# Chunked retention ahead of two feed-forward layers: k is loaded once and turned on TensorE, the lo parts of the converted weights move to VectorE, and the conversion gets a new pace

## The chip, the cores and the metric

The kernel runs on one core of a Trainium2 chip. The metric is device time in microseconds (us). The kernel before has a median of 803.65 us over 3 runs (802.65 to 805.5). Times below that come from the trace belong to one more, profiled execution of the same program, which took 802.34 us, 800.3 us of it in the profiled span.

## The reference

What is computed, cut to what matters:

```python
# 1 attention: 4 batches, 8 heads, 576 positions, head size 64; the decay replaces a softmax
ret = (q @ k.T / 8) * where(i >= j, gamma[h] ** (i - j), 0)
x   = (ret @ v)                      # laid out as 2304 tokens x 512
# 2 a gated product of two projections; the weights come as float64
x   = ((x @ w_a) * (x @ w_b)) @ w_out          # 512 -> 1536 -> 512
# 3 a mixture of 8 experts, one expert for each token
e   = argmax(x @ w_gate + modality_bias[modality_id])
out = softmax_weight * (relu(x @ w1[e]) @ w2[e])    # 512 -> 1024 -> 512
```

## The kernel before, in words

Every engine works off a list whose order is that of the code (the scheduler is off). Big tiles are `unit`s of 4 KB in each of the 128 partitions, of which there are 40, and a load on SyncE's queue (SP) waits until the unit that it gets is free. PSUM has 8 banks.

**Attention** goes over 20 chunks of 64 or 128 positions (5 for each batch: one of 64, then four of 128), with a state that is carried from chunk to chunk. For chunk i, `a_load` fetches `qk` (q and k, both already transposed on the host) and `kv` (k and v as rows, so k comes twice). `a_scale` on GpSimd (POOL) multiplies q and k by decays. `a_scores` on TensorE (PE) makes the scores, `a_mask` on VectorE (DVE) writes the carried state times a decay into a block-diagonal tile `sbd` (L358) and multiplies the scores by the decay mask (L366), `a_inter`, `a_state` and `a_intra` on PE make the output and the next state, and `a_hi`/`a_lo` write the output out of PSUM. One pass of the loop, here called a step, holds the scores of chunk i+1 and everything else of chunk i. The first steps hold `warm`, matmuls on constants.

**Conversion.** The weights of part 2 are float64; a piece is 128 x 512 of them, and there are 36 (w_a, w_b and w_out for each of 12 groups fc). `Conv.step(new)` moves each piece under way on by one stage and starts `new` others. The stages: load (SP); nothing; absolute value on ScalarE (ACT, L262); four instructions on DVE that put a float32 together from the two halves (L265, L269, L273, L277; called the four below); the hi part on ACT (L284, rounded to float32r) and the lo part, value minus hi, on POOL (L285). The attention steps named in `CV_AT` start one piece each, 8 in all; from then on each step of part 2 starts two (`CV_MOE`), over 14 steps.

**Part 2** goes in steps of one token group (384 tokens) and one fc. In a step `gemm1` makes two products in PSUM (L565), the first of which ACT copies out (`a`); DVE multiplies the second by it (`g`, L573), ACT rounds that (`gh`), DVE subtracts (`gl`, L577); `gemm2` of the step before follows on PE (L585). The first two token groups alternate (8 fc each), so the pieces are used as they are converted. Their six accumulators leave two PSUM banks, so the second product of a step can't start before `g` of the step before it has been read out. Hooks in the steps issue conversion, set-up (`setup` at step 1) and the routing weights (`load_gate` at step 18).

Of the kernel before, what the change touches and what calls it, by code (L numbers as in the profile page):

```python
# [9 lines left out]
F32 = mybir.dt.float32  # L10
# [40 lines left out]
def _const_parts():  # L51
    g = 1.0 - 2.0 ** (-5.0 - np.arange(H))
    i = np.arange(P)
    rel = i[None, :] - i[:, None]
    mask = np.where(
        rel[:, None, :] >= 0,
        g[None, :, None] ** np.maximum(rel, 0)[:, None, :],
        0.0,
    ) / np.sqrt(D)
    mask = mask.reshape(P, NP, 2, P).transpose(0, 2, 1, 3)  # L60
    gp = np.repeat(g.reshape(NP, 2).T, D, axis=0)
    qt = gp[:, :, None] ** i[None, None, :] / np.sqrt(D)
    kt = np.zeros((P, 5, H))
    st = np.zeros((P, 5, NP))
    for c, s0 in enumerate(STARTS):
        kt[:, c, :] = g[None, :] ** (-(s0 + i)[:, None].astype(float))
        st[:, c, :] = gp ** float(s0)
    one = np.ones((P, 1))
    parts_a = [("mask", mask), ("kt", kt), ("st", st), ("qt", qt)]
    parts_b = [  # L70
        ("tri", (rel > 0).astype(float)),
        ("ident", np.eye(P)),
        ("iota8", one * np.arange(NE)[None, :]),
        ("base0", one * (np.arange(NE) * NTOK)[None, :]),
        ("tok", i[:, None] + P * np.arange(NTT)[None, :]),
        ("thr0", one * (NT * np.arange(7) + NS)[None, :]),
        ("thr1", one * (NT * np.arange(7))[None, :]),
        ("sid", one * (np.arange(MAXS) - EARLYS * 1.0)[None, :]),
        ("jp", i[:, None] + P * np.arange(TPC)[None, :]),
    ]  # L80
    return parts_a, parts_b
# [18 lines left out]
def build(  # L100
    ctx: ExitStack,
    tc: tile.TileContext,
    qkf,
    kv,
    wab,
    wout,
# [46 lines left out]
    def unit(name, shape, dt=F32):  # L153
        return up.tile(shape, dt, name=name, tag="u")
# [44 lines left out]
            nc.tensor.matmul(ps, lhsT=ones, rhs=wide, start=True, stop=True)  # L199

    def setup():
        nc.sync.dma_start(out=cb, in_=cstb)
        nc.gpsimd.tensor_copy(tri, cb_("tri"))
        nc.gpsimd.tensor_copy(base, cb_("base0"))

        zt = unit("zt", [P, NE * NTT * 2])
        nc.gpsimd.memset(zt, 0.0)
        nc.gpsimd.dma_start(out=perm.rearrange("(p a) o -> p (a o)", p=P), in_=zt)


# [21 lines left out]
    class Conv:  # L232
# [23 lines left out]
        def advance(self, c):  # L256
            c["n"] += 1
            i, raw = c["i"], c["raw"]
            fc, j = divmod(i, 3)
            if c["n"] == 2:  # L260
                t = c["t"] = unit(f"cv{i}", [P, 512], U32)
                nc.scalar.activation(out=t.bitcast(F32), in_=raw[:, :, 1].bitcast(F32), func=AF.Abs)  # L262
            elif c["n"] == 3:
                t = c["t"]
                nc.vector.tensor_scalar(  # L265
                    out=t.bitcast(F32), in0=t.bitcast(F32), scalar1=k1, scalar2=k2,
                    op0=ALU.max, op1=ALU.min,
                )
# [12 lines left out]
            elif c["n"] == 4:  # L281
                t = c["t"]
                w = wts[fc][j] = unit(f"w{fc}_{j}", [P, 2, 512], F32R)
                nc.scalar.copy(w[:, 0, :], t.bitcast(F32))  # L284
                nc.gpsimd.tensor_sub(w[:, 1, :], t.bitcast(F32), w[:, 0, :].bitcast(F32))  # L285
                self.live.remove(c)


# [8 lines left out]
        return [xp.tile([P, KC, NT], F32, name=f"xf{n}", tag="x")]  # L297

    chunks = [(b, c) for b in BATCHES for c in range(5)]
    offs = np.cumsum([0] + [P * 8 * SIZES[c] for b, c in chunks])  # L300
    A = [dict() for _ in chunks]

    def geo(i):
        b, c = chunks[i]
        return b, c, SIZES[c], b * S + STARTS[c]

    def a_load(i, what=("qk", "kv")):
        b, c, n, r0 = geo(i)
        if "qk" in what:
            qk = unit(f"qk{i}", [P, 2 * NP * P])[:, : 2 * NP * n]  # L310
            nc.sync.dma_start(
                out=qk, in_=qkf[int(offs[i]) : int(offs[i + 1])].rearrange("(p f) -> p f", p=P)
            )
            A[i]["qk"] = qk.rearrange("p (t a s) -> p t a s", t=2, a=NP)
        if "kv" in what:
            A[i]["kv"] = unit(f"kv{i}", [P, 2, DM])
            nc.sync.dma_start(
                out=A[i]["kv"][:n], in_=kv[r0 : r0 + n, :].rearrange("r (t d) -> r t d", t=2)
            )

    def a_scale(i):
        b, c, n, r0 = geo(i)
# [2 lines left out]
        A[i]["qs"] = qks[:, 0, :].rearrange("p (a s) -> p a s", a=NP)  # L325
        A[i]["ks"] = qks[:, 1, :]
        if c > 0:
            nc.gpsimd.tensor_mul(A[i]["qs"][:, :, :n], qk[:, 0, :, :n], qt[:, :, :n])
        if c < 4:
            nc.gpsimd.tensor_mul(  # L330
                qks[:n, 1, :].rearrange("p (h d) -> p h d", h=H),
# [19 lines left out]

    def a_mask(i):
        b, c, n, r0 = geo(i)
        if c > 0:
            A[i]["S"] = sbd[i % 2]
            for hf in range(2):
                sl = slice(D * hf, D * hf + D)
                nc.vector.tensor_mul(  # L358
                    sbd[i % 2][sl, :, sl],
                    A[i - 1]["Sp"][sl, :, :],  # L360
                    st[sl, c, :].unsqueeze(2).to_broadcast([D, NP, D]),
                )
        rt = unit(f"rt{i}", [P, 2, NP, P])
        A[i]["rt"] = rt
        for hf in range(2):
            nc.vector.tensor_mul(  # L366
                rt[:n, hf, :, :n], A[i]["sc"][hf][:n, :, :n], mask[:n, hf, :, :n]
            )

    def a_state(i):  # L370
        b, c, n, r0 = geo(i)
# [73 lines left out]
    n_ch = len(chunks)
    a_load(0, ["qk"])
    a_load(1, ["qk"])
    a_load(0, ["kv"])
# [740 lines left out]
```

## Time and profile before

| | |
|---|---|
| time, median of 3 runs | 803.65 us (802.65 to 805.5) |
| the profiled execution's own time | 802.34 us |
| its span | 800.3 us |
| PE busy | 755.3 us (94%) |
| DVE busy | 492.0 us (61%) |
| ACT busy | 245.1 us (31%) |
| POOL busy | 200.1 us (25%) |

The shares of busy time are means over parts with different limits: attention lies at the start (some 87 us), conversion beside the first steps of part 2 follows (to about 219 us), then part 2 without conversion, then the experts. A share of 94% for PE says little of either of the first two.

### The profile page before, as it was taken

Reading aid. Unit: us, or ns where it says so; the run is one execution under the profiler, and the core shown is the slowest. Engines: PE = TensorE matmul, PEld = TensorE weight load, DVE = VectorE, ACT = ScalarE, POOL = GpSimd, SP = SyncE. Lnnn points to the kernel's source line nnn. Section 1 sums busy time; section 2 is a strip of 40 time slices with the busy share of each in tenths; the row PEclk is TensorE's granted clock in tenths of the full one; section 3 lists DMA queues with packets and bytes.
Section 4 is the critical chain, followed back from the end, with each engine's and each line's share of the span. In section 5 each row is a group of like instructions: output and inputs, shape, how many; then the busy total and the mean of one; then the engine's idle time right before and its main releaser. Section 6 shows DMA issues by size and latency. Waiting matters only on the chain.

```text
span 800.3 us, 12194 instructions
## 1 busy us (share of the span) xinstructions
PE 755.3 (94%) x4610; PEld 686.1 (86%) x4610; DVE 492.0 (61%) x1212; ACT 245.1 (31%) x461; POOL 200.1 (25%) x213
## 2 busy tenths in 40 slices
PE   8888999878899999999999999999999999999992
PEld 6777998767798899999999999999978999999992
DVE  3799458989839664454445545856896844444610
ACT  1232233334321311221122112215434435344621
POOL 4576313424213210030003000113115133140302
PEclk9999999999999999999999999999999999999997
DMA  9999702322041100100020001034746385465201
GB/s 323 400 364 409 247 25 82 106 81 77 1 185 39 41 1 1 45 36 0 1 80 1 1 1 39 2 101 151 288 139 152 101 295 168 131 200 160 80 1 44
DMA packets 27908, 91.99 MB, mean 115 GB/s; under 512 B 4543, under 2 KB 4703, under 8 KB 27840
## 3 DMA queue, kind: packets, MB, share of 16 engines
q1 hardware_dynamic: 22928, 79.11, 28.6%
q0 software_dynamic: 4336, 9.92, 4.0%
q10 hardware_dynamic: 576, 2.10, 0.7%
q8 instruction: 38, 0.62, 0.3%
q14 instruction: 30, 0.25, 0.1%
HBM read 78.36 MB, written 13.01 MB: 114 GB/s over the span
## 4 chain that ended last, share of the span: by engine, by line
PE 65%; DVE 18%; issue 7%; DMA 5%; POOL 1%; ACT 1%; SPq 1%; POOLq 0%; DVEq 0%; ACTq 0%
PE ab L565 30%; PE acc L585 15%; PE h L849 9%; PE y L866 9%; DVE cv L273 4%; DVE cv L269 3%; DMA raw<-in_wab_dram 3%; DMA qk<-in_qkf_dram 2%; DVE scr L502 2%; DVE cv L265 1%; DVE cv L277 1%; DVE g L573 1%; DVE el L783 1%; ACT gh L575 1%; DVE gl L577 1%
## 5 line engine op out<-in xcount | busy, mean ns | idle before, releaser
L565 PE MATMUL ab<-xh,w 128*128 128x384 f32 x1152 | 277.5, 337 | 16.2 <-DVE g L573 14.2
L565 PEld LDWEIGHTS ab<-xh,w 128*128 128x128 f32 x1152 | 208.2, 188 | 26.0 <-DVE g L573 17.7
L565 PE MATMUL ab<-xl,w 128*128 128x384 f32 x576 | 162.6, 336 | 0.0
L573 DVE TENSOR_TENSOR g<-ab,a 128x384 f32<-128x384 f32 x72 | 40.0, 556 | 124.2 <-ACT a L571 99.0
L585 PE MATMUL acc<-w,gh 128*128 128x512 f32 x432 | 113.1, 397 | 1.2 <-ACT gh L575 1.2
L502 DVE SCALAR_TENSOR_TENSOR scr<-row,wg 128x512 f32<-128x512 f32 x144 | 104.6, 729 | 4.7 <-ACT row L489 0.5
L565 PEld LDWEIGHTS ab<-xl,w 128*128 128x128 f32 x576 | 105.4, 188 | 0.9
L585 PEld LDWEIGHTS acc<-w,gh 128*128 128x128 f32 x432 | 79.0, 188 | 14.2 <-ACT gh L575 1.5
L571 ACT COPY a<-ab 128x384 f32<-128x384 f32 x72 | 34.3, 476 | 184.4 <-PE ab L565 181.8
L575 ACT CAST gh<-g 128x384 fp32r<-128x384 f32 x72 | 36.9, 513 | 131.0 <-DVE g L573 130.4
L285 POOL TENSOR_TENSOR w<-cv,w 128x512 fp32r<-128x512 f32 x36 | 50.9, 1432 | 103.1 <-DVE gl L577 81.4
L783 DVE TENSOR_TENSOR el<-er,eh 128x1024 fp32r<-128x1024 f32 x56 | 67.9, 1224 | 12.5 <-ACT eh L782 11.8
L545 POOL DMA_INDIRECT perm<-tg,ix x18 | 18.4, 1020 | 224.3 <-DVE ix L543 187.9
L856 DVE SCALAR_TENSOR_TENSOR hl<-h,hh 128x384 fp32r<-128x384 f32 x48 | 26.7, 556 | 67.8 <-ACT hh L854 61.4
L577 DVE TENSOR_TENSOR gl<-g,gh 128x384 fp32r<-128x384 f32 x72 | 40.2, 558 | 41.7 <-ACT gh L575 41.1
L849 PE MATMUL h<-sl,eh 128*128 128x384 f32 x192 | 64.6, 336 | 0.2 <-DVE sl L830 0.2
L849 PE MATMUL h<-sh,el 128*128 128x384 f32 x192 | 64.7, 337 | 0.0
L849 PE MATMUL h<-sh,eh 128*128 128x384 f32 x192 | 64.6, 337 | 0.0
L585 PE MATMUL acc<-w,gl 128*128 128x512 f32 x216 | 61.4, 392 | 0.0
L782 ACT CAST eh<-er 128x1024 fp32r<-128x1024 f32 x56 | 57.5, 1041 | 2.4 <-DMA er<-in_w1r_dram 2.4
L854 ACT ACTIVATE hh<-h 128x384 fp32r<-128x384 f32 x48 | 23.6, 491 | 97.0 <-PE h L849 76.7
L585 PEld LDWEIGHTS acc<-w,gl 128*128 128x128 f32 x216 | 40.6, 188 | 9.3
(160 smaller groups left out, 1016.5 us busy)
## 6 DMA issues: line engine op xcount, KB each, us to landing
er<-in_w1r_dram SPq DMA_DIRECT2D x28, 512.0 KB
er<-in_w2r_dram SPq DMA_DIRECT2D x28, 512.0 KB
raw<-in_wab_dram SPq DMA_DIRECT2D x24, 512.0 KB
qk<-in_qkf_dram SPq DMA_DIRECT2D x16, 512.0 KB
kv<-in_kv_dram SPq DMA_DIRECT2D x16, 512.0 KB
raw<-in_wout_dram SPq DMA_DIRECT2D x12, 512.0 KB
x2d<-row SPq DMA_DIRECT2D x18, 256.0 KB
xsp<-xf SPq DMA_DIRECT2D x4, 768.0 KB
```

Source lines behind the costliest of these rows:

```text
L285: nc.gpsimd.tensor_sub(w[:, 1, :], t.bitcast(F32), w[:, 0, :].bitcast(F32))
L502: nc.vector.scalar_tensor_tensor(out=scr, in0=row, scalar=1.0, in1=wg[e // 2][:, e % 2, :], op0=ALU.mult, op1=ALU.mult, accum_out=R["l"][: ...
L565: nc.tensor.matmul(ps[j], lhsT=ws[j][:, wi, k, :], rhs=x[:, k, :], start=(k == 0 and q == 0), stop=(k == KC - 1 and q == 2),)
L571: nc.scalar.copy(a, ps[0])
L573: nc.vector.tensor_mul(g, ps[1], a)
L575: nc.scalar.copy(gh, g)
L577: nc.vector.tensor_sub(gl, g, gh.bitcast(F32))
L585: nc.tensor.matmul(accs[t], lhsT=x[:, t * P : (t + 1) * P], rhs=w[:, wi, :], start=(fc == 0 and q == 0), stop=(fc == NFA - 1 and q == 2),)
L782: nc.scalar.copy(hi, raw)
L783: nc.vector.tensor_sub(lo, raw, hi.bitcast(F32))
L849: nc.tensor.matmul(ps, lhsT=w[:, fc % 2, k, :], rhs=x[:, k, :], start=(k == 0 and q == 0), stop=(k == KC - 1 and q == 2),)
L866: nc.tensor.matmul(y, lhsT=x[:, t * P : (t + 1) * P], rhs=w, start=(fc == 0 and q == 0), stop=(fc == NFF - 1 and q == 2),)
```

## The change

- `qk` becomes a load of q alone (`qf`, half the bytes). k is turned on PE: `a_turn` transposes the four 128-column blocks of k out of `kv` into a PSUM bank `kT`, and ACT copies that beside q. In the loop the turn of chunk i+2 stands between the scores of chunk i+1 and `a_inter` of chunk i.
- The state goes into `sbd` by two plain copies on ACT (`a_blocks`) in place of two multiplications on DVE. The decay that they applied is put into the factor for q: `qtc`, two more units, filled by POOL once for each of the four chunks of the first batch.
- L285, the lo part of a piece, becomes a DVE instruction (L284 in the new file).
- `CV_ATT` goes from 8 pieces to 10, started at steps 2, 3, 4, 6, 7, 8, 11, 12, 13 and 16; part 2 starts 2, 1, 2, 1, 2, 2, 1, 2, 2, 2, 2, 1, 2, 2, 2 pieces (26) in place of 2 in each of 14 steps.
- Loads run four chunks ahead, not three; `cstb` with the identity for the transposes is the first load, and the routing weights' loads go from ACT's queue to SP's.

```diff
-    CV_ATT = 8
-    CV_AT = (3, 6, 7, 8, 11, 12, 13, 16)
+    CV_ATT = 10
+    CV_AT = (2, 3, 4, 6, 7, 8, 11, 12, 13, 16)
-    CV_MOE = (2,)
+    CV_MOE = (2, 1, 2, 1, 2, 2, 1, 2, 2, 2, 2, 1, 2, 2, 2, 0)
...
-                nc.gpsimd.tensor_sub(w[:, 1, :], t.bitcast(F32), w[:, 0, :].bitcast(F32))
+                nc.vector.tensor_sub(w[:, 1, :], t.bitcast(F32), w[:, 0, :].bitcast(F32))
...
+    def a_turn(i):
+        b, c, n, r0 = geo(i)
+        ps = bank(f"kT{i}", [P, NP, P])
+        for p in range(NP):
+            nc.tensor.transpose(
+                ps[:, p, :n], A[i]["kv"][:n, 0, p * P : (p + 1) * P], ident[:n, :n]
+            )
+        nc.scalar.copy(A[i]["qk"][:, 1, :, :n], ps[:, :, :n])
...
-            nc.gpsimd.tensor_mul(A[i]["qs"][:, :, :n], qk[:, 0, :, :n], qt[:, :, :n])
+            dec = qtc[(c - 1) // 2][:, (c - 1) % 2]
+            if b == BATCHES[0]:
+                nc.gpsimd.tensor_mul(dec, qt, st[:, c, :].unsqueeze(2).to_broadcast([P, NP, P]))
+            nc.gpsimd.tensor_mul(A[i]["qs"][:, :, :n], qk[:, 0, :, :n], dec[:, :, :n])
...
-                nc.vector.tensor_mul(
-                    sbd[i % 2][sl, :, sl],
-                    A[i - 1]["Sp"][sl, :, :],
-                    st[sl, c, :].unsqueeze(2).to_broadcast([D, NP, D]),
-                )
...
+            nc.scalar.copy(sbd[i % 2][sl, :, sl], A[i - 1]["Sp"][sl, :, :])
...
+    nc.sync.dma_start(out=cb, in_=cstb)
+    a_load(0)
+    a_load(1, ["kv"])
     nc.sync.dma_start(out=ca, in_=csta[:, 8 * P :])
     nc.sync.dma_start(out=mask.rearrange("p a b c -> p (a b c)"), in_=csta[:, 0 : 8 * P])
-    a_load(2, ["qk"])
-    a_load(1, ["kv"])
-    a_load(2, ["kv"])
+    a_load(1, ["q"])
+    a_load(2)
...
+        if 1 <= i and i + 2 < n_ch:
+            a_turn(i + 2)
         if 0 <= i < n_ch:
             a_inter(i)
             a_state(i)
+            a_blocks(i + 1)
             a_intra(i)
             a_hi(i)
```

What the change does to PE's list is seen in an attention step of the first batch (step 2: `sc` are scores, `o` the output, `S` the state, `kT` the turned k). Before, from the last score of chunk 3 to the first of the next chunk:

```order
L344 MATMUL sc_1_231<-qk_134 128x128
L392 MATMUL o_245<-qks_183,sbd 128x128 x4
L378 MATMUL S_160<-kv_113,qks_183 64x64 x8
L403 MATMUL o_245<-rt_242,kv_113 64x128 x8
L344 MATMUL sc_0_273<-qk_179 128x128
```

And in the changed kernel, the same stretch of the same engine:

```order
L360 MATMUL sc_1_267<-qk_118 128x128
L326 MATMUL kT_281<-cb,kv_155 128x128 x4
L408 MATMUL o_287<-qks_211,sbd 128x128 x4
L394 MATMUL S_180<-kv_116,qks_211 64x64 x8
L419 MATMUL o_287<-rt_276,kv_116 64x128 x8
L360 MATMUL sc_0_318<-qk_153 128x128
```

Four transposes stand in front of the product with `sbd`; the rest keeps its order.

On DVE the place is a step of part 2 with conversion (the third and fourth piece are under way; `g`, `gl` as above, `cv` a piece, `w` its parts). Before, `gl` is followed by the four of the first piece, and then by those of a second one:

```order
L573 TENSOR_TENSOR g_3_1435<-ab_3_1_1408,a_3_1421 128x384
L577 TENSOR_TENSOR gl_3_1439<-g_3_1435,gh_3_1437 128x384
L265 TENSOR_SCALAR cv_1390<-cv_1390 128x512
L269 TENSOR_SCALAR cv_1390<-cv_1390 128x512
L273 SCALAR_TENSOR_TENSOR cv_1390<-raw_1264,cv_1390 128x512
L277 SCALAR_TENSOR_TENSOR cv_1390<-raw_1264,cv_1390 128x512
```

In the changed kernel a step of that stretch (step 4, where two pieces are finished and one is put together):

```order
L597 TENSOR_TENSOR g_2_1447<-ab_2_1_1420,a_2_1433 128x384
L601 TENSOR_TENSOR gl_2_1451<-g_2_1447,gh_2_1449 128x384
L284 TENSOR_TENSOR w_1_1453<-cv_1344,w_1_1453 128x512
L284 TENSOR_TENSOR w_2_1456<-cv_1346,w_2_1456 128x512
L264 TENSOR_SCALAR cv_1406<-cv_1406 128x512
L268 TENSOR_SCALAR cv_1406<-cv_1406 128x512
L272 SCALAR_TENSOR_TENSOR cv_1406<-raw_1280,cv_1406 128x512
L276 SCALAR_TENSOR_TENSOR cv_1406<-raw_1280,cv_1406 128x512
```

The lo parts (`w` from `cv` and `w`) now stand on DVE behind `gl`, and the number of the four changes from step to step.

On ACT the place is the attention steps around chunks 7 and 8 (`xf` is the output, `cv` and `w` belong to the conversion). Before:

```order
L423 COPY xf_487<-o_466 128x4x128
L284 CAST w_0_510<-cv_411 128x512
L262 ACTIVATE cv_513<-raw_413 128x512
L423 COPY xf_487<-o_517 128x4x128
L262 ACTIVATE cv_564<-raw_464 128x512
```

In the changed kernel, one step of it:

```order
L283 CAST w_1_596<-cv_480 128x512
L261 ACTIVATE cv_603<-raw_482 128x512
L329 COPY qk_456<-kT_607 128x4x64
L384 COPY sbd<-S_436 64x4x64 x2
L439 COPY xf_575<-o_613 128x4x128
```

The copies of the turned k and of the state stand behind the hi part of a piece, which waits for the four of that piece on DVE.

## Rows read from the trace of the kernel before

**Rows 1.** Windows: length, busy us of PE, PEld, DVE, ACT, POOL; clock; DMA share; GB/s

```profile
30.00:80.00 50.00, 41.53 (x594) 35.97 (x590) 47.63 (x74) 14.31 (x27) 32.28 (x25) 0.93 1.03 388
52.00:58.00 6.00, 4.73 (x50) 4.31 (x52) 5.84 (x11) 1.41 (x3) 3.90 (x3) 0.72 1.06 292
105.00:219.00 114.00, 98.25 (x499) 87.82 (x497) 100.22 (x141) 41.74 (x81) 37.98 (x26) 1.00 0.21 65
```

**Rows 2.** The chain that ended last, in order of time: start us, us, what

```profile
86.55 8.55 PE ab L565 x48
...
219.41 2.37 PE ab L565 x12
221.78 2.08 PE acc L585 x9
223.86 4.18 PE ab L565 x24
```

**Rows 3.** Timeline of DVE and POOL in one conversion step: start us, us

```profile
114.00 0.56 DVE L573 TENSOR_TENSOR g<-ab,a 128x384 f32<-128x384 f32 x1
...
115.14 0.56 DVE L577 TENSOR_TENSOR gl<-g,gh 128x384 fp32r<-128x384 f32 x1 [0.58 <-ACT gh L575]
115.61 0.42 DVE L265 TENSOR_SCALAR cv<-cv 128x512 f32<-128x512 f32 x1
115.70 2.92 POOL L285 TENSOR_TENSOR w<-cv,w 128x512 fp32r<-128x512 f32 x2 [19.69 <-DVE gl L577]
...
116.07 1.42 DVE L269 TENSOR_SCALAR cv<-cv 128x512 uint32<-128x512 uint32 x1
...
117.52 1.66 DVE L273 SCALAR_TENSOR_TENSOR cv<-raw,cv 128x512 uint32<-128x512 uint32 x1
...
119.21 0.69 DVE L277 SCALAR_TENSOR_TENSOR cv<-raw,cv 128x512 uint32<-128x512 uint32 x1
119.81 0.42 DVE L265 TENSOR_SCALAR cv<-cv 128x512 f32<-128x512 f32 x1
...
122.07 0.55 DVE L573 TENSOR_TENSOR g<-ab,a 128x384 f32<-128x384 f32 x1
```

**Rows 4.** Timeline of the attention: scores on PE, first k scaling on POOL

```profile
6.80 1.16 PE L344 MATMUL sc<-qk 64*128 64x128 f32 x16
...
7.41 1.03 POOL L330 TENSOR_TENSOR qks<-kv,ca 64x512 f32<-64x512 f32 x1 [6.00 <-DMA ca<-in_csta_dram]
...
17.80 1.16 PE L344 MATMUL sc<-qk 64*128 64x128 f32 x16 [0.30 <-DMA qk<-in_qkf_dram]
...
21.47 0.68 PE L344 MATMUL sc<-qk 64*64 64x64 f32 x16
...
24.20 1.16 PE L344 MATMUL sc<-qk 64*128 64x128 f32 x16
...
26.73 1.16 PE L344 MATMUL sc<-qk 64*128 64x128 f32 x16 [0.29 <-DMA qk<-in_qkf_dram]
```

**Rows 5.** Groups by line, attention only (to 86.5 us): count, busy us, mean ns

```profile
L366 DVE TENSOR_TENSOR rt<-sc,mask 128x512 f32<-128x512 f32 x32 | 20.6, 687 | 0.5
...
L358 DVE TENSOR_TENSOR sbd<-S,ca 64x256 f32<-64x256 f32 x32 | 13.4, 420 | 10.4 <-PE S L378 10.1
...
L273 DVE SCALAR_TENSOR_TENSOR cv<-raw,cv 128x512 uint32<-128x512 uint32 x8 | 8.2, 1021 | 0.3
L269 DVE TENSOR_SCALAR cv<-cv 128x512 uint32<-128x512 uint32 x8 | 7.5, 940 | 0.3
...
L277 DVE SCALAR_TENSOR_TENSOR cv<-raw,cv 128x512 uint32<-128x512 uint32 x7 | 6.7, 963 | 0.2
...
L265 DVE TENSOR_SCALAR cv<-cv 128x512 f32<-128x512 f32 x8 | 5.2, 644 | 0.0
...
L429 DVE TENSOR_TENSOR xl<-o,xh 128x512 fp32r<-128x512 f32 x4 | 2.7, 682 | 0.1
```

**Rows 6.** Instructions of one tile: transposes in an expert slot, ns min/median/max, first to last start

```profile
L839 PE MATMUL xT<-cb,xg x4: 270/272/273, 756.4 to 756.7; 128*128 128x128 f32 x4
```

More of the change, by code (lines that the diff above doesn't have):

```diff
@@ L70, in _const_parts @@
     parts_b = [
+        ("ident", np.eye(P)),
         ("tri", (rel > 0).astype(float)),
-        ("ident", np.eye(P)),
         ("iota8", one * np.arange(NE)[None, :]),
@@ L102, in build @@
     tc: tile.TileContext,
-    qkf,
+    qf,
     kv,
@@ L201, in setup @@
     def setup():
-        nc.sync.dma_start(out=cb, in_=cstb)
         nc.gpsimd.tensor_copy(tri, cb_("tri"))
@@ L299, in build @@
     chunks = [(b, c) for b in BATCHES for c in range(5)]
-    offs = np.cumsum([0] + [P * 8 * SIZES[c] for b, c in chunks])
+    n_ch = len(chunks)
+    offs = np.cumsum([0] + [P * NP * SIZES[c] for b, c in chunks])
     A = [dict() for _ in chunks]
@@ L305, in geo, with a_load @@
         return b, c, SIZES[c], b * S + STARTS[c]
-    def a_load(i, what=("qk", "kv")):
+    def a_load(i, what=("kv", "q")):
         b, c, n, r0 = geo(i)
-        if "qk" in what:
-            qk = unit(f"qk{i}", [P, 2 * NP * P])[:, : 2 * NP * n]
+        if "q" in what:
+            A[i]["qk"] = unit(f"qk{i}", [P, 2, NP, P])
             nc.sync.dma_start(
-                out=qk, in_=qkf[int(offs[i]) : int(offs[i + 1])].rearrange("(p f) -> p f", p=P)
+                out=A[i]["qk"][:, 0, :, :n],
+                in_=qf[int(offs[i]) : int(offs[i + 1])].rearrange("(p a s) -> p a s", p=P, a=NP),
             )
-            A[i]["qk"] = qk.rearrange("p (t a s) -> p t a s", t=2, a=NP)
         if "kv" in what:
@@ L319, in a_load @@
             )
+    def a_turn(i):
[6 more added lines that the diff above has]
+        nc.scalar.copy(A[i]["qk"][:, 1, :, :n], ps[:, :, :n])
+    qtc = [unit(f"qtc{j}", [P, 2, NP, P]) for j in range(2)]
     def a_scale(i):
@@ L353, in a_mask @@
         b, c, n, r0 = geo(i)
[L354 to L357, printed above, removed]
-                nc.vector.tensor_mul(
-                    sbd[i % 2][sl, :, sl],
-                    A[i - 1]["Sp"][sl, :, :],
-                    st[sl, c, :].unsqueeze(2).to_broadcast([D, NP, D]),
-                )
         rt = unit(f"rt{i}", [P, 2, NP, P])
@@ L368, in a_mask, with a_blocks @@
             )
+    def a_blocks(i):
+        if i >= n_ch or chunks[i][1] == 0:
+            return
+        A[i]["S"] = sbd[i % 2]
+        for hf in range(2):
+            sl = slice(D * hf, D * hf + D)
+            nc.scalar.copy(sbd[i % 2][sl, :, sl], A[i - 1]["Sp"][sl, :, :])
     def a_state(i):
@@ L444, in build @@
     cv = Conv()
[L445 to L448, printed above, removed]
+    nc.sync.dma_start(out=cb, in_=cstb)
+    a_load(0)
+    a_load(1, ["kv"])
     nc.sync.dma_start(out=ca, in_=csta[:, 8 * P :])
     nc.sync.dma_start(out=mask.rearrange("p a b c -> p (a b c)"), in_=csta[:, 0 : 8 * P])
-    a_load(2, ["qk"])
-    a_load(1, ["kv"])
-    a_load(2, ["kv"])
+    a_load(1, ["q"])
+    a_load(2)
     for i in range(-1, n_ch + 1):
-        if 3 <= i + 3 < n_ch:
-            a_load(i + 3)
+        if 3 <= i + 4 < n_ch:
+            a_load(i + 4)
+        if i + 1 < len(WARM):
+            warm(WARM[i + 1])
+        if i == -1:
+            a_turn(0)
+            a_turn(1)
         if 0 <= i + 1 < n_ch:
             a_scale(i + 1)
-            if i + 1 < len(WARM):
-                warm(WARM[i + 1])
             a_scores(i + 1)
@@ L471, in build @@
             a_state(i)
+            a_blocks(i + 1)
             a_intra(i)
             a_hi(i)
+        if i == 0:
+            a_turn(2)
     wg = []
@@ L480, in load_gate @@
             t = unit(f"wg{j}", [P, 2, DM])
-            nc.scalar.dma_start(
+            nc.sync.dma_start(
                 out=t.rearrange("p a d -> p (a d)"),
@@ L1141, in _arrays @@
     q, k, v = i["q"], i["k"], i["v"]
-    qk = np.stack([q, k], 0).transpose(1, 2, 4, 0, 3).reshape(B, NP, P, 2, S)
-    qk = qk.transpose(0, 2, 3, 1, 4)
-    qkf = np.concatenate(
+    qd = q.transpose(0, 1, 3, 2).reshape(B, NP, P, S).transpose(0, 2, 1, 3)
+    qf = np.concatenate(
         [
-            qk[b, :, :, :, s0 : s0 + n].ravel()
+            qd[b, :, :, s0 : s0 + n].ravel()
             for b in BATCHES
@@ L1156, in _arrays @@
     return {
-        "qkf": c(qkf),
+        "qf": c(qf),
         "kv": c(kv),
```

## Prediction, made before the changed kernel was run

> **What bounds the kernel now.** I read the windows first, to see which engine is full in which part, then the chain of waits, then the timeline of one step of each of the two parts that the change touches. In the part with conversion, from 105 to 219 us, DVE is busy 100.22 of 114 us, PE only 98.25, at a granted clock of 1.00 (2.4 GHz) [rows 1]. The chain of waits shows what an undisturbed step costs PE: 4.18 for gemm1 and 2.08 for gemm2, 6.26 to 6.27 us [rows 2]. The timeline shows a step that takes 8.07 us from one `g` to the next (114.00 to 122.07) [rows 3], and it is DVE's list that fills it. So this part goes at DVE's pace.
>
> Why a DVE step is that long is to be seen in the same group. The second piece's four take 2.26 us (119.81 to 122.07). The first piece's take 4.20 (115.61 to 119.81), because L269 and L273, 0.43 and 0.69 when POOL is idle, take 1.42 and 1.66 while POOL does its two subtractions (2.92 us) [rows 3]. The collision costs 1.94 us in each step; without it the step would be 6.13, under PE's 6.27.
>
> How much that costs in all: undisturbed, step 18 would reach its second product at 86.55 + 4.18 + 17 x 6.27 + 2.09 = 199.4 us. It reached it at 219.41 [rows 2]. **20.0 us** are lost there.
>
> In attention the bound is less plain. From 30 to 80 us DVE is busy 47.63 of 50 us, PE 41.53, POOL 32.28, and the DMA engines are full (388 GB/s) [rows 1]. The scores of full chunks stand 3.67 us apart when nothing waits (17.80 to 21.47) [rows 4]; the stage as a whole takes much longer than its PE work. DVE bounds it once conversion has begun; DMA holds the scores up for 0.3 us at a time [rows 4].
>
> **The conversion steps of part 2.** The lo parts leave POOL, so the collision (1.94) goes, and DVE gets one more instruction of 128x512 with two SBUF inputs for each piece. This one isn't in the trace. Its neighbour L277, same width, one input more, takes 0.69 when POOL is idle; `gl`, 384 wide, takes 0.56 [rows 3]. I take 0.70, with bounds 0.60 and 0.74 (0.56 x 512/384). A step with x pieces in the four and y lo parts costs DVE 1.61 (`g` to the first of the four, 114.00 to 115.61) + 2.26x + 0.70y. Two and two: 7.53. A piece started in step s is in the four at s+3 and has its lo part at s+4, so the list 2, 1, 2, 1, 2, 2, 1, 2, 2, 2, 2, 1, 2, 2, 2 gives DVE, from step 3 on: 6.13, 5.27, 6.83, 5.27, 6.83, 7.53, 5.27, 6.83, 7.53, 7.53, 7.53, 5.27, 6.83, 7.53, 7.53.
>
> PE's 6.27 stands against each. `g` may come late by gemm2 + one product - its own length = 2.08 + 2.09 - 0.56 = 3.6 us before PE waits for the PSUM bank. Carrying the lag from step to step: 0.6, 0, 0.6, 1.8, 0.8, 1.4, 2.6, and then the limit is passed by 0.3, 1.3, 0.8 and 1.3 us in steps 12, 13, 16 and 17. In step 19 PE needs the lo part of piece 34, which stands 2.3 us into a step that is 3.6 late, and waits 1.3 more. Sum of waits: **5.0 us** (3.1 with 0.60, 5.8 with 0.74). What is late next is only this. So the part gives back 20.0 - 5.0 = **15.0 us** (14.2 to 16.9). After step 19 nothing differs: the routing loads, now queued on SP behind the last weight loads, are wanted only when the first token group is finished, and one of them still waits for the unit of piece 35's last lo part, as it waited for POOL's.
>
> **Attention, start.** The first scores of chunk 1 stood at 6.80 [rows 4]. Now they need q of chunk 1, which is queued behind 2,111 KB (161 + 128 + 256 + 512 + 286 + 512 + 256). `ca`, before the end of 1,310 KB, was used at 7.41 [rows 4]; 801 KB more at 388 GB/s [rows 1] are 2.1 us, so 9.5, and the four `warm` matmuls stand in front of them behind the first turn: I take 10.2, a delay of 3.4 us.
>
> **Attention, PE.** A turn of 4 transposes starts one every 0.14 us or so (4 from 756.4 to 756.7, 0.27 each) [rows 6]: 0.57, and some 0.35 for a chunk of 64. A full step goes from 3.67 to 4.24. Scores of chunk 6 move from 24.20 to 24.20 + 3.4 + 2.6 for five turns - 0.7 of waits for the old q and k loads = 29.5 [rows 4]. A batch is then 3 x 3.67 + 2.73 (21.47 to 24.20) + 2.24 (24.20 to 26.73, less the wait of 0.29) + 2.6 for turns = 18.6 us of PE [rows 4]. Three batches are left, and the last steps have 1.8 us less in them (no turns, no scores): left alone, PE would end at 29.5 + 55.8 - 1.8 = 83.5, three us sooner than the 86.55 of before [rows 2].
>
> **Attention, DVE.** The 32 writes to `sbd` go to ACT (13.4 us less) [rows 5], which was busy 14.31 of 50 us [rows 1]. In come 2 more pieces and 9 lo parts before the last mask. The four cost 0.64 + 0.94 + 1.02 + 0.96 = 3.57 a piece here [rows 5] against 2.26 alone: POOL was busy 65% of the time [rows 1]. With L285 gone from POOL I estimate 49% of the time, so 2.26 + 1.31 x 49/65 = 3.2 for the four, and by the same share 0.95 for a lo part, which is between 0.69 (POOL idle) and 1.66 (L273 beside POOL) [rows 3]. From the first mask after which conversion runs without a break (chunk 6, at 29.5 + 1.09 = 30.6) to the last: 12 pairs of full masks at 1.29 (20.6/16) and two short ones 17.0, nine fours 28.8, nine lo parts 8.6, the outputs' lo halves 2.9 [rows 5] - 57.3 us, so 87.9; one product more, 1.03, and attention ends at 88.9, **2.4 us later**. Bounds: if POOL never gets in the way PE decides, 83.5 (-3.0); with 3.57 and 0.95 to 1.66 it is 92 to 98 (+6 to +12). ACT's new copies (20 of k, 32 of the state) fill idle time, but they stand behind the hi part of a piece, which waits for DVE: that wait is the way in which DVE's lag reaches the scores.
>
> DMA moves 4.7 MB less (12 us of full engines at 388 GB/s [rows 1]); as DVE is the bound, I count it as nothing. POOL's four extra decays, about as long as one of its subtractions (1.46) [rows 3], lie in the first batch, where a step of 4.24 has room for them beside the two scalings.
>
> **The rule that speaks against this.** A DVE instruction with two SBUF inputs beside POOL: L273 takes 1.66, not 0.69 [rows 3]. The Trainium skill, "SBUF — State Buffer", section "Who interferes with whom", says that such an instruction contends with a GpSimd instruction that reads SBUF, and that whichever issues second is blocked until the other is through. The trace agrees: the surplus, 0.97, is less than one of POOL's subtractions (1.46). By this rule moving the lo part can't collide in part 2, where POOL is left idle, and can in attention, where POOL goes on scaling; that is the upper bound above.
>
> **Sum.** 802.34 - 15.0 + 2.4 = 789.7 us against this execution's own time. It lies 1.3 us below the median of the runs, so I say 790.
>
> **Rivals.**
> *Attention hardly collides.* POOL runs ahead of DVE, as its inputs are loaded four chunks early. Then attention ends between 83.5 and 86.5: 802.3 - 15.5 - 1.5 = 785. For it: POOL loses its subtractions, ten us of work at 1.46. Against: DVE was full [rows 1].
> *The lo parts are blocked in attention.* +6 to +12: 802.3 - 15 + 9 = 796. For it: the 1.66 of L273.
> *The clock falls, and it gets slower.* In 52 to 58 us the granted clock averaged 0.72, so part of it at the lower level (1.2 GHz), in a stretch in which PE was busy only 4.73 of 6 us [rows 1]. Such a fall costs some 1.7 us (0.28 x 6). If the turns do not keep the clock up, it could fall again and again: from 8 falls on (12.6/1.7) the gain is gone, and with 13 the time is 802.3 - 12.6 + 22 = 812. The Trainium skill, "TensorE: Matmul & The Clock Gate", Part 4, says that transposes don't count as PE-busy the way matmuls do; no run here shows it yet. Against it: the turns are 0.57 of 4.24 us.
> *It does not do what it says:* if the lo part costs DVE 1.3 us in part 2, the part loses its 20 us again, and the time is 802.3 + 2.4 = 805. Nothing in the rows is that slow with POOL idle.
>
> **How the numbers follow.** The forecast, 786 to 794 us: 0.55. Attention without collisions, 781 to 786: 0.19. Blocked lo parts, 794 to 800: 0.16. The clock, 803 and up: 0.05. No gain in part 2: 0.05. Runs of this kernel lie within some 0.3% of each other, 2.4 us, which is what I call the same. The range for 8 in 10 takes in the first two and most of the third: 781 to 798. Faster: 0.55 + 0.19 + 0.16 + a little of the last = 0.92; same 0.03, slower 0.05.
>
> **What would show it.** Steps with two and two pieces 7.3 to 7.6 us from `g` to `g`, those with fewer near 6.27; L269 at 0.43 in part 2; waits of PE on `g` about 4 us in place of 20; the first gemm1 of part 2 at 87 to 91 us; DVE full from about 35 us to there; lo parts in attention at about 1 us; scores of chunk 1 at about 10. I am wrong if attention grows by more than 6 us, if `g` to `g` stays near 8, or if a new wait, on ACT's copies of k or the state, leads the list.

## The result, and the profile after

The changed kernel takes 791.53 us (median of 4 runs, 791.01 to 794.47) against 804.45 for the kernel before, timed beside it (median of 4 runs): ratio 0.985, 95% interval 0.982 to 0.988. The forecast was 790 (781 to 798), faster. The profiled execution took 794.47 us, with a span of 792.6.

I cut each span at the first and the last start of a gemm1 weight product: attention, part 2, and the rest. Before: 86.5 + 471.3 + 242.5 = 800.3. After: 92.3 + 456.7 + 243.6 = 792.6. So part 2 gives back 14.6 us (forecast 15.0), attention takes 5.8 more (forecast 2.4), the rest 1.1 more (forecast 0).

The windows after, columns as in [rows 1], with a stretch of attention in the middle:

```profile
30.00:80.00 50.00, 45.17 (x623) 39.43 (x622) 43.55 (x60) 26.54 (x58) 23.41 (x18) 0.93 0.84 292
55.00:62.00 7.00, 6.75 (x58) 6.18 (x60) 5.67 (x11) 2.04 (x4) 0.00 (x0) 0.52 1.04 317
105.00:219.00 114.00, 111.11 (x574) 103.14 (x573) 90.21 (x164) 45.12 (x87) 0.00 (x0) 0.99 0.23 75
```

From 105 to 219 us PE has gone from 98.25 to 111.11 us busy, and POOL does nothing. From 30 to 80 us DVE is no longer full (43.55 of 50), and PE has 45.17 in place of 41.53. From 55 to 62 us the granted clock is 0.52: nearly all of it at the lower level.

A step of part 2 after, on DVE, two pieces and two lo parts; it answers to [rows 3]:

```profile
145.39 0.55 DVE L597 TENSOR_TENSOR g<-ab,a 128x384 f32<-128x384 f32 x1
146.52 0.56 DVE L601 TENSOR_TENSOR gl<-g,gh 128x384 fp32r<-128x384 f32 x1 [0.58 <-ACT gh L599]
147.04 1.29 DVE L284 TENSOR_TENSOR w<-cv,w 128x512 fp32r<-128x512 f32 x2
148.25 0.42 DVE L264 TENSOR_SCALAR cv<-cv 128x512 f32<-128x512 f32 x1
148.71 0.43 DVE L268 TENSOR_SCALAR cv<-cv 128x512 uint32<-128x512 uint32 x1
149.17 0.69 DVE L272 SCALAR_TENSOR_TENSOR cv<-raw,cv 128x512 uint32<-128x512 uint32 x1
149.89 0.69 DVE L276 SCALAR_TENSOR_TENSOR cv<-raw,cv 128x512 uint32<-128x512 uint32 x1
...
152.75 0.55 DVE L597 TENSOR_TENSOR g<-ab,a 128x384 f32<-128x384 f32 x1
```

The collision is gone: L268 and L272, the old L269 and L273, take 0.43 and 0.69 where they took 1.42 and 1.66. From `g` to `g` it is 7.36 us (before 8.07). Two lo parts need 1.21 us from the start of the first to the start of the next instruction (147.04 to 148.25), 0.60 each.

PE in attention after; it answers to [rows 4] and the first row of [rows 2]:

```profile
10.77 1.23 PE L360 MATMUL sc<-qk 64*128 64x128 f32 x16
...
29.50 1.16 PE L360 MATMUL sc<-qk 64*128 64x128 f32 x16
...
40.38 1.16 PE L360 MATMUL sc<-qk 64*128 64x128 f32 x16
...
43.83 0.43 PE L419 MATMUL o<-rt,kv 128*64 128x128 f32 x2 [0.34 <-DVE rt L373]
...
45.44 0.68 PE L360 MATMUL sc<-qk 64*64 64x64 f32 x16
...
49.54 0.43 PE L419 MATMUL o<-rt,kv 128*64 128x128 f32 x2 [1.94 <-DVE rt L373]
...
51.16 1.16 PE L360 MATMUL sc<-qk 64*128 64x128 f32 x16
...
55.25 1.35 PE L419 MATMUL o<-rt,kv 64*64 64x64 f32 x16 [1.74 <-DVE rt L373]
56.53 2.08 PE L360 MATMUL sc<-qk 64*128 64x128 f32 x16
...
63.15 1.16 PE L360 MATMUL sc<-qk 64*128 64x128 f32 x16
...
67.22 1.16 PE L360 MATMUL sc<-qk 64*128 64x128 f32 x16
...
72.24 0.68 PE L360 MATMUL sc<-qk 64*64 64x64 f32 x16
...
91.12 1.25 PE L419 MATMUL o<-rt,kv 128*64 128x128 f32 x16
...
92.30 0.45 PE L589 MATMUL ab<-xh,w 128*128 128x384 f32 x1
```

Chunk 1 is scored at 10.77 (forecast 10.2), chunk 6 at 29.50 (29.5). What follows is not as I had it: two waits of almost 2 us for the masked scores, then scores that take 2.08 instead of 1.16 us.

The waits of PE in attention after (us in total, times, longest):

```profile
PE o L419 <- DVE rt L373: 4.8, 7, 1.9
PE kT L326 <- DMA kv<-in_kv_dram: 2.6, 2, 1.9
```

And the end of part 2's loss, step 19, on DVE, ACT and PE:

```profile
213.32 0.55 DVE L597 TENSOR_TENSOR g<-ab,a 128x384 f32<-128x384 f32 x1
...
213.90 0.51 ACT L599 CAST gh<-g 128x384 fp32r<-128x384 f32 x1 [5.43 <-DVE g L597]
214.32 1.13 ACT L283 CAST w<-cv 128x512 fp32r<-128x512 f32 x2
...
214.99 0.45 PE L589 MATMUL ab<-xh,w 128*128 128x384 f32 x1 [1.89 <-ACT w L283]
```

PE waits 1.89 us for the hi part of piece 34. That copy has had its input since 211.15 us, when the four of piece 34 ended, but stands on ACT behind `gh`, and `gh` waits for `g`, which DVE makes late.

### The profile page after: what moved, and what is told of

Read it like the earlier page. It is cut to its first block, busy times and chain, and to the rows that moved or that the text cites. A ratio compares the mean times of both kernels' runs of the same rounds, so it can differ in the third digit from the quotient of the medians.

```text
span 792.6 us, 12370 instructions
## 1 busy us (share of the span) xinstructions
PE 762.7 (96%) x4690; PEld 695.8 (88%) x4690; DVE 476.2 (60%) x1216; ACT 267.1 (34%) x513; POOL 157.1 (20%) x181
## 4 chain that ended last, share of the span: by engine, by line
PE 75%; DVE 13%; issue 7%; ACT 2%; POOL 1%; DMA 1%; SPq 0%; POOLq 0%; DVEq 0%; ACTq 0%
PE ab L589 32%; PE acc L609 16%; PE y L890 9%; PE h L873 9%; DVE cv L272 2%; DVE w L284 2%; PE sc L360 2%; PE o L419 2%; DVE cv L268 2%; DVE scr L526 1%; PE o L408 1%; DVE cv L264 1%; PE kT L326 1%; DVE g L597 1%; PE S L394 1%
## 5 line engine op out<-in xcount | busy, mean ns | idle before, releaser
L1014 POOL TENSOR_TENSOR xl<-xl,xh 128x384 fp32r<-128x384 f32 x16 | 19.9, 1263 | 183.2 <-ACT xh L1013 183.1
```

## The experiments

My theory after the first look: in part 2 the collision with POOL was the loss. In attention PE is the bound; DVE delays it only where fours stand close together, and the clock falls behind such waits. The rival: DVE's sum of work bounds attention, as I had forecast. Part 2 is from the first to the last start of a gemm1 weight product, as above; its loss is against 451.1 us, its length when every step takes PE's 6.27 us (before: 471.3 less the 20.2 that its steps take more). "Rest" is what follows the last gemm1. First gemm1, part 2 and rest are of one profiled execution of each kernel, the median of 4 to 10 executions. e1 to e4, e5 to e8 and e9 to e11 ran on three chips, each group beside the kernel before: across groups, compare the ratios.

| kernel | first gemm1 | part 2 | rest | median | ratio (95%) |
|---|---|---|---|---|---|
| before | 86.5 | 471.3 | 242.5 | 802.9 to 804.5 | |
| e1 changed, again | 91.5 | 455.1 | 242.3 | 790.78 | 0.983 (0.980-0.986) |
| e2 lo parts on POOL | 88.3 | 462.6 | 243.9 | 797.48 | 0.992 (0.990-0.995) |
| e3 only lo parts on DVE | 89.4 | 462.2 | 242.5 | 796.25 | 0.990 (0.987-0.993) |
| e4 only the new attention | 87.9 | 471.2 | 243.7 | 804.26 | 1.001 (0.999-1.003) |
| e5 changed, pieces spread | 89.5 | 455.2 | 243.9 | 790.87 | 0.984 (0.982-0.987) |
| e6 changed, two a step | 91.7 | 461.1 | 242.7 | 797.59 | 0.993 (0.991-0.995) |
| e7 changed, 11 in attention | 94.3 | 452.6 | 242.7 | 791.61 | 0.986 (0.983-0.989) |
| e9 lo on POOL in attention only | 88.1 | 455.1 | 243.8 | 788.51 | 0.983 (0.981-0.984) |
| e10 as e9, spread | 87.0 | 456.7 | 242.4 | 787.68 | 0.981 (0.979-0.982) |
| e11 as e10, 11 pieces | 90.8 | 452.7 | 243.7 | 788.86 | 0.982 (0.980-0.984) |

**e1, the changed kernel again.** No edit.

> The changed kernel itself once more, nothing edited: a second execution in profile. My theory of its first profile: PE alone would end attention at 83.5 us; the 8.8 us up to 92.3 are 4.8 us of waits for the masked scores (DVE takes two or three pieces in a row) and some 3.2 us of one fall of the granted clock at 55 to 62 us that follows such waits. The waits lie in the order of the work, so they must come again: 4 to 6 us of waits of the intra products for L373, first gemm1 at 88 us (no fall) to 93 us (a fall). Part 2: loss up to step 19 some 5.5 us with a fall there, 3.5 without. Time 791.5 against the kernel before 804.4, ratio 0.985. Rival: the waits were chance of one execution; then they are under 2 us here and the first gemm1 stands at 85 to 86.

The waits for L373 come again, 4.7 us, and a fall of the clock behind them (granted clock 0.51 from 57 to 60.5 us); the first gemm1 is at 91.5. The wait of 1.9 us in step 19 comes again too, but no fall behind it. The same six microseconds in the changed kernel, and in its second execution:

```profile
214.00:220.00 6.00, 4.91 (x16) 4.46 (x17) 2.37 (x4) 1.85 (x5) 0.00 (x0) 0.72 0.86 260
```

```profile
214.00:220.00 6.00, 5.71 (x28) 4.99 (x29) 2.58 (x5) 1.54 (x4) 0.00 (x0) 1.00 0.74 261
```

So the waits lie in the order of the work; whether the clock falls behind one of them differs from execution to execution. The loss of part 2 is 4.0 us here and 5.6 there.

**e2, lo parts back on POOL.**

```diff
-                nc.vector.tensor_sub(w[:, 1, :], ...)
+                nc.gpsimd.tensor_sub(w[:, 1, :], ...)
```

> The changed kernel with one line undone: the lo parts are on POOL again, the pace and the new attention stay. My theory (the collision of POOL's subtraction with L268 and L272 on DVE is what the change took away): steps with two and two pieces go from 7.36 back to about 8.07 us from g to g, those with one lo part from 6.76 to about 7.1, one and two from 5.12 to 5.8; over 14 such steps 8.4 us, less the early ones' slack: part 2 about 7 us longer than in the changed kernel. In attention DVE has 4.08 us a piece (3.17 for the four and 0.91 for the lo part) and gets 3.57: the waits for the masked scores fall by 1 to 2 us, and the first gemm1 comes at 86 to 91. Time 793 to 797. Rival, the pace alone did it: g to g stays under 7.5 in steps of two and two, and the time is 790 to 792.

One step of part 2 in this kernel, DVE and POOL:

```profile
163.02 0.55 DVE L597 TENSOR_TENSOR g<-ab,a 128x384 f32<-128x384 f32 x1
...
164.71 2.93 POOL L284 TENSOR_TENSOR w<-cv,w 128x512 fp32r<-128x512 f32 x2 [5.60 <-DVE gl L601]
...
165.07 1.41 DVE L268 TENSOR_SCALAR cv<-cv 128x512 uint32<-128x512 uint32 x1
166.52 1.67 DVE L272 SCALAR_TENSOR_TENSOR cv<-raw,cv 128x512 uint32<-128x512 uint32 x1
...
171.08 0.55 DVE L597 TENSOR_TENSOR g<-ab,a 128x384 f32<-128x384 f32 x1
```

8.06 us from `g` to `g`; steps with one lo part 7.08, with one piece and two lo parts 5.80. Part 2 is 5.9 to 7.5 us longer than in the changed kernel. That is the collision, put back by one line. Attention is 3.2 to 4.0 us shorter. The time, 797.5, is half a microsecond above what I expected.

**e3, the kernel before with lo parts on DVE and nothing else.**

```diff
-                nc.gpsimd.tensor_sub(w[:, 1, :], ...)
+                nc.vector.tensor_sub(w[:, 1, :], ...)
```

> The kernel before with one line changed: the lo parts on DVE; pace 2 and the old attention stay. My theory: steps of part 2 go from 8.07 to 7.36 us (12 to 14 of them, 8.5 to 10 us back of the 20.0), so DVE stays the bound there; in attention seven lo parts at 0.9 go in and the four get 0.4 shorter each: +3 to +4 us. Time 804.4 - 9 + 3.5 = 799. Rival A, lo parts blocked by POOL in attention (1.66 each): 803 to 805. Rival B, the lo part on DVE is all of the gain: 791 to 793.

Steps of 7.37 us; part 2 gives back 9.1, attention takes 2.9 more. This one line is over half of the change's gain, and not all of it; rival B falls, and rival A as well. I expected 799, counted from 804.4; it is 796.3, beside 803.1 for the kernel before.

**e4, the new attention alone.**

```diff
-    CV_ATT = 10 ... CV_MOE = (2, 1, 2, 1, ...)
+    CV_ATT = 8 ... CV_MOE = (2,)
-                nc.vector.tensor_sub(w[:, 1, :], ...)
+                nc.gpsimd.tensor_sub(w[:, 1, :], ...)
```

> The new attention alone (k loaded once and turned, state copies on ACT, decays on POOL), with the conversion as in the kernel before: eight pieces, lo parts on POOL, two a step in part 2. My theory: part 2 loses its 20.0 us as before (8.07 a step); attention is bound by PE with 2 to 4 us of waits for DVE, as eight pieces at 3.57 are 28.6 us of DVE work against 40.8 in the changed kernel, and ends at 85 to 88 instead of 86.55. Time 803 to 806, the same as before. Rival, the turns cost more than they give: attention ends over 90, time over 808. Rival, the load saved is worth its 12 us of DMA: attention ends under 83, time under 800.

Part 2 is as before (8.06 a step, 471.2), attention is within the bracket, the time the same as before. Without the rest of the change, the turns, the copies on ACT and the 4.7 MB that are not loaded come to nothing. No run has the lo parts on DVE and the new pace with the old attention, so what the new attention is worth beside them isn't shown.

**e5, the same ten pieces spread over attention.**

```diff
-    CV_AT = (2, 3, 4, 6, 7, 8, 11, 12, 13, 16)
+    CV_AT = (1, 2, 4, 6, 8, 9, 12, 13, 14, 16)
```

> The changed kernel with the same ten pieces in attention, started in steps 1, 2, 4, 6, 8, 9, 12, 13, 14, 16 instead of 2, 3, 4, 6, 7, 8, 11, 12, 13, 16, so that no more than two fours stand in steps that follow each other in the second batch. My theory (PE would bound attention; the waits for the masked scores come from fours in a row, and the fall of the clock from the waits): waits of the intra products for L373 1 to 2 us instead of 4.7, no fall or a short one, first gemm1 at 86 to 88 instead of 91.5 to 92.3; time 786 to 788 against 791 for the changed kernel. Rival, DVE's sum of work decides, not its order: first gemm1 still at 91 or later, time 790 to 792.

Half a miss. The waits fall to 3.4 us (expected 1 to 2), one fall of the clock stays (54 to 57 us), the first gemm1 comes at 89.5, and the time is not better: in the profiled executions attention is 2.0 us shorter than in e1, but the rest is 1.6 longer, by a fall of the clock (see the end). The DVE rows show something odd, an L264 that took 3.94 us where it takes 0.42 alone:

```profile
25.03 1.27 POOL L344 TENSOR_TENSOR qks<-qk,qtc 128x512 f32<-128x512 f32 x1
25.88 3.94 DVE L264 TENSOR_SCALAR cv<-cv 128x512 f32<-128x512 f32 x1
...
28.50 1.04 POOL L346 TENSOR_TENSOR qks<-kv,ca 128x512 f32<-128x512 f32 x1
```

POOL worked without a pause from 22.80 to 29.54 us, and L264 ended 0.28 us later. It doesn't explain the miss: DVE stood idle for 1.08 us before 34.68, so it had caught up, and PE follows the pace of e8 until 50 us.

**e6, two pieces in every step of part 2.**

```diff
-    CV_MOE = (2, 1, 2, 1, 2, 2, 1, 2, 2, 2, 2, 1, 2, 2, 2, 0)
+    CV_MOE = (2,)
```

> The changed kernel with two pieces in every step of part 2, as before, instead of the list of twos and ones. My theory: twelve steps of two and two at 7.36 us against PE's 6.27 put DVE 13.1 us behind, of which 3.6 are slack: 9.5 us of waits on g; the last piece is there two steps sooner, so the wait of 1.9 us for its hi part in step 19 goes, with the fall of the clock behind it. Part 2 about 4 to 6 us longer than in the changed kernel, 460 to 461; time 795 to 797. Rival, the pace is worth nothing once the lo parts are on DVE: 790 to 792.

Part 2 is 461.1 and so loses 10.0 us, of which the rows show 7.3 as waits on `g`; its steps are 7.37: the pace of ones and twos is worth 4.4 to 6 us, and the time, 797.6, is just above the bracket.

**e7, an eleventh piece in attention.**

```diff
-    CV_ATT = 10
+    CV_ATT = 11
-    CV_AT = (2, 3, 4, 6, 7, 8, 11, 12, 13, 16)
+    CV_AT = (2, 3, 4, 6, 7, 8, 11, 12, 13, 14, 16)
-    CV_MOE = (..., 1, 2, 2, 2, 0)
+    CV_MOE = (..., 1, 2, 2, 1, 0)
```

> The changed kernel with one piece more in attention (started in step 14, where DVE has idle time) and one less in the last 2 of the pace (a 1), so that the second weight of the last tile is a step earlier. My theory: in the changed kernel PE waits in step 19 1.9 us for the hi part of that piece, because the copy stands on ACT behind gh, which waits for g; now both go, and with them any fall of the clock there (1.8 us in one of two profiles); the piece in attention costs 0 to 1 us as PE bounds the last batch. Part 2 2 to 4 us shorter, time 787 to 789. Rival, the wait is passed on to a later product, or attention grows by the piece's 4 us: 791 or more.

The wait on ACT's copy in step 19 is gone and part 2 is 2.5 us shorter than in e1, but the fours now stand close together at the end of attention, a new wait of 1.87 us for L373 comes at 92.7 us, and attention takes 2.8 us more. The rival wins: no change.

**e8, no conversion in attention.** The ten pieces are converted behind it, so only attention is to be read from this kernel.

```diff
-    CV_ATT = 10
-    CV_AT = (2, 3, 4, 6, 7, 8, 11, 12, 13, 16)
+    CV_ATT = 0
+    CV_AT = ()
...
+    for new in (2, 2, 2, 2, 2, 0, 0, 0, 0):
+        cv.step(new)
```

> The changed kernel with no conversion in attention; the ten pieces are converted in a row between attention and the first gemm1, so part 2 begins late and only attention is to be read. My theory: PE alone bounds attention, with no waits on DVE after chunk 6; the last product ends at 83 to 84.5 us (83.5 by the sum of the prediction), and the granted clock does not fall after the start, as the turns keep PE busy like products. Rival, the turns let the clock fall: falls of the clock come although PE has no waits, and the end is at 86 or later. Rival, DMA bounds: waits for kv or q of over 2 us after chunk 6.

The scores of chunks 6 and 9 to 15, the output's second product of chunk 8 (44.73) and the last product of attention, and the windows of the same stretch:

```profile
30.91 1.16 PE L360 MATMUL sc<-qk 64*128 64x128 f32 x16
...
41.80 1.16 PE L360 MATMUL sc<-qk 64*128 64x128 f32 x16
...
44.73 1.05 PE L419 MATMUL o<-rt,kv 128*64 128x128 f32 x16
45.70 0.68 PE L360 MATMUL sc<-qk 64*64 64x64 f32 x16
...
48.82 1.16 PE L360 MATMUL sc<-qk 64*128 64x128 f32 x16
...
51.58 1.16 PE L360 MATMUL sc<-qk 64*128 64x128 f32 x16
...
55.64 1.16 PE L360 MATMUL sc<-qk 64*128 64x128 f32 x16
...
59.70 1.16 PE L360 MATMUL sc<-qk 64*128 64x128 f32 x16
...
63.61 0.68 PE L360 MATMUL sc<-qk 64*64 64x64 f32 x16
...
82.49 1.09 PE L419 MATMUL o<-rt,kv 128*64 128x128 f32 x16
```

```profile
24.00:83.00 59.00, 58.91 (x902) 52.63 (x904) 22.16 (x38) 27.14 (x60) 27.16 (x28) 1.00 0.79 273
```

Attention ends at 83.58 us, PE is busy 58.91 of 59 us and the granted clock is 1.00. So without conversion PE bounds attention, and the turns do not bring the clock down. This kernel leaves out the loads of the ten pieces too, so for the DMA engines the changed kernel itself has to be asked: its two waits for DMA, 2.6 us, both end by 7.2 us, so they are no bound after that.

**e9 to e11, lo parts where they cost least.** The pieces of attention have their lo part on POOL, the others on DVE; e10 also spreads the ten pieces as e5 does; e11 has eleven, started in steps 1, 2, 4, 6, 8, 9, 11, 12, 13, 14 and 16, with e7's pace.

```diff
-                nc.vector.tensor_sub(w[:, 1, :], ...)
+                (nc.gpsimd if i < CV_ATT else nc.vector).tensor_sub(w[:, 1, :], ...)
```

> The changed kernel with the lo parts of the ten pieces of attention on POOL and all later ones on DVE. My theory (a lo part belongs on DVE where POOL is idle, and on POOL where POOL collides with DVE anyway): attention as with all lo parts on POOL, first gemm1 at 88 to 89 us instead of 91.5 to 92.3; part 2 as in the changed kernel, 455 to 457; time 787 to 788.5. Rival, the gains of the two places don't add, since part 2 begins with DVE further behind: 790 to 792.

> As the last, and the ten pieces of attention started in steps 1, 2, 4, 6, 8, 9, 12, 13, 14, 16. My theory: DVE has 3.57 us a piece instead of 4.08 and no three in a row, so the waits for the masked scores are 1 to 2 us, first gemm1 at 86 to 88; time 785.5 to 788. Rival, spreading gives nothing of its own: the same as the last, 787 to 788.5.

> As the last, with an eleventh piece in attention (steps 1, 2, 4, 6, 8, 9, 11, 12, 13, 14, 16) and a 1 in place of the last 2 of the pace. My theory: part 2 2.5 to 4 us shorter, as the wait of step 19 for the copy on ACT goes (seen when the eleventh piece was added alone: 452.6), attention 1 to 2.5 us longer (2.8 alone): the same as the last or up to 2 us less, 785 to 787.5. Rival, attention pays the whole piece, 3.6 us: slower than the last by 1 or more.

e9 joins the attention of e2 (88.1; e2 88.3) to the part 2 of the changed kernel (455.1), as I expected. In e10 the waits for L373 are 2.0 us, attention ends at 87.0 with no fall in it. e10 has the lowest median, 787.68; its interval and that of e9 overlap, but its five runs (786.23 to 787.91) all lie below e9's five (788.38 to 789.94) on the same chip, so spreading is worth some 0.8 us there. e11 pays in attention (+3.8) what it gains in part 2 (-4.0) and misses its bracket, though in part it is the clock that these two profiles compare: e11's attention holds a fall (0.51 from 70 to 77 us), e10's step 19 another (0.66 from 210 to 215); by median it is 1.2 us slower than e10, with intervals that overlap. e10 is the fastest version seen: 3 to 4 us by median under the changed kernel, which ran on other chips; its interval lies at the edge of that of the first comparison (0.982 to 0.988) and overlaps e1's.

## Why the prediction was right, and where its steps were wrong

**The collision: right.** L268 and L272 are at 0.43 and 0.69, steps of two and two at 7.36 (7.3 to 7.6 said), and one line puts 8.06 back (e2). The Trainium skill, "SBUF — State Buffer", section "Who interferes with whom", which I weighed there, holds in part 2: POOL idle, no stretched instruction.

**Part 2's 15.0 us: right as a sum, its two parts off against each other.** A lo part costs DVE 0.60 in a row of instructions, not 0.70, so `g` is late by less: e7, which has no wait in step 19, loses 1.5 us in part 2 (452.6 less 451.1), and its rows there name `g` alone, where I had 3.7. Step 19 cost more: of e1's 4.0 lost that leaves 2.5, not 1.3, and PE waits there first for the hi part (1.9), not for the lo part on DVE, since the copy is queued on ACT behind `gh`. I had looked at DVE's list only. Behind it the clock fell in one of two executions: the ten products from 215.71 took 3.57 us, about 1.8 more than the 0.17 each of those ahead.

**The pace and the move, apart.** Both are needed: without the move 462.6 (e2), without the list 461.1 (e6), with both 455.1 to 456.7.

**The start of attention and PE's own time: right, with luck in both numbers.** Chunk 6 came at 29.50 as forecast, but chunk 1 0.6 us later than said (10.77) and the way from there 0.6 shorter; in e1, e5 and e8 chunk 6 comes at 30.4 to 30.9. PE alone was put at 83.5 and ends at 83.58 in e8, where chunk 6 came 1.4 us later and a full step is 4.06 us (scores at 33.67 and 37.73), not 4.24. A turn was put at 0.57, which counts the last transpose to its end; the four of [rows 6] start within 0.3 us, and the step grew by 0.39 (from 3.67).

**The end of attention: the step that failed.** I took DVE's list from 30.6 us on as without gaps and let its sum, 87.9 at the last mask, set the end, at 88.9. The prices were right: in attention the four cost 0.51 + 0.65 + 0.93 + 1.09 = 3.17 (3.2 said), a lo part 0.91 (0.95 said). Groups of DVE up to 93 us, which answer to [rows 5]:

```profile
L276 DVE SCALAR_TENSOR_TENSOR cv<-raw,cv 128x512 uint32<-128x512 uint32 x9 | 9.8, 1089 | 0.3
L272 DVE SCALAR_TENSOR_TENSOR cv<-raw,cv 128x512 uint32<-128x512 uint32 x10 | 9.3, 931 | 0.3
L284 DVE TENSOR_TENSOR w<-cv,w 128x512 fp32r<-128x512 f32 x9 | 8.2, 914 | 4.8 <-ACT w L283 4.7
L268 DVE TENSOR_SCALAR cv<-cv 128x512 uint32<-128x512 uint32 x10 | 6.5, 646 | 0.3
L264 DVE TENSOR_SCALAR cv<-cv 128x512 f32<-128x512 f32 x10 | 5.1, 509 | 0.0
```

But DVE isn't full: it stands 4.8 us before lo parts alone, for hi parts that stand on ACT behind copies of what PE has yet to make. Its work from the first of these masks (30.86) to the last (91.22) is 54.6 us, 2.7 less than I had; the list still ends 3.3 us later, because of idle time that my sum didn't have. A list of work that comes in bunches is late where it is dense and idle where it is thin.

What sets the end is PE and what it loses. That is seen by laying its scores beside those of e8, from one chunk's to the next's, in us:

| from the scores of chunk | changed kernel | e8 | longer by |
|---|---|---|---|
| 9 to 10 | 5.06 | 3.90 | 1.2 |
| 10 to 11 | 5.72 | 3.12 | 2.6 |
| 11 to 12 | 5.37 | 2.76 | 2.6 |
| 12 to 13 | 6.62 | 4.06 | 2.6 |
| 14 to 15 | 5.02 | 3.91 | 1.1 |

These 10.0 us are all of it: from the scores of chunk 6 to the last product it is 61.62 us (29.50 to 91.12), in e8 51.58 (30.91 to 82.49). The fall of the clock is some 3.3 of them: from 55.25 to 63.15, 7.90 us for what takes 4.63 in e8 (51.01 to 55.64). The other 6.8 lie at the waits for L373, which the other four rows hold. The rows of waits show only 4.8 of these, mainly because a product that waited starts on the first half of its masked scores and waits again inside: it takes 1.61 us (43.83 to 45.44) where e8 takes 0.97 (44.73 to 45.70). In e1 the same comparison gives 8.5 us, with a shorter fall, and in e10 2.4. The forecast's sum has no term for these waits and none for the clock behind them.

**Rivals.** *Attention hardly collides*: no, the fours cost 3.17, not 2.26; but the bound it named, PE at 83.5, is the real one. *The lo parts are blocked*: they are at times (0.69 or 1.57), and their move to POOL brings 3 us of attention back (e2, e9), though the fours get dearer then (3.80 a piece). *The clock falls*: it did, and cost some 1.3 to 3.3 us each time, but behind waits and not because of the turns: the kernel before, without any, has three falls in attention (0.57 from 54 to 58, 0.51 from 68 to 71.5, 0.52 from 81.5 to 85 us). By the rule that I cited (the Trainium skill, "TensorE: Matmul & The Clock Gate", Part 4: transposes don't count as busy the way matmuls do) they might have let it fall, and in e8, with a turn in nearly each step and a clock of 1.00, they don't. Why one wait has a fall behind it and another none stays open. *It does not do what it says*: excluded by e2 and e3.

**The total.** 802.34 - 14.6 + 5.8 + 1.1 = 794.6 for the profiled execution. In the second one fewer falls of the clock leave 802.34 - 16.2 + 5.0 - 0.2 = 790.9, where the medians lie (791.5 and 790.8). So 790 came out with the term of part 2 right and that of attention 2.6 to 3.4 too small; part 2's own 15.0 lay between the 14.6 and the 16.2 seen. Attention's 5.8 stayed just under the 6 us that I had named as a sign of being wrong.

## What to carry to other kernels

Where DVE works off bunches of another stream's work between instructions that PE waits for, the sum of its busy time doesn't give the end: lay its list against the moments at which PE needs each result, and look at the in-order queue of the engine between them too (here ACT's copy behind `gh`). An elementwise instruction is best placed stage by stage: the same subtraction is cheap on DVE where GpSimd is idle, and better on GpSimd where the two collide anyway (e9: part 2 7.5 us under e2's, attention 3.4 under e1's). And a wait of PE of one or two microseconds can cost as much again in clock, in some executions and not in others (of the five profiles with 1.9 us in step 19, the changed kernel's first and e10's have a fall behind it), so compare more than one profile before a difference of 2 us gets a cause.

## What the runs showed that I had not expected

- A DVE instruction with a single SBUF input, in place, can be held up by POOL for longer than one of POOL's instructions: L264, 0.42 alone, took 3.94 us beside a POOL that worked without a pause (e5), whose instructions took 1.03 to 1.27 us. That such a form is held up at all stands in [rows 3] already (L269, 1.42 in place of 0.43). The Trainium skill, "SBUF — State Buffer", section "Who interferes with whom", says so of such forms too, if they run in the mode that uses the shared ports, and has them blocked for one instruction of GpSimd; here it was more than three, and no run tells which mode it was.
- The rest of the program, which the change doesn't touch, takes 242.3 to 242.7 us or 243.6 to 243.9. The longer value comes where the granted clock falls behind the wait of 1.9 us for `sl`, some 37 us after the last gemm1 (seen in the changed kernel's first profile, e2, e4, e5, e9, e11), the shorter where it doesn't (before, e1, e3, e6, e7, e10).
